# Forward first stages at every second place, and earlier statistics, norms and folds of the last slabs, in a fused Fourier-filter and GEGLU kernel on one Trainium2 core

## The chip, the core and the metric

The kernel runs on one core of a Trainium2 chip. The core has a matrix engine (TensorE, "PE" in the profile, with its weight loads as "PEld"), a vector engine (VectorE, "DVE"), an engine for activation functions (ScalarE, "ACT"), a general engine (GpSimd, "POOL") and SyncE ("SP"), which in this kernel issues every DMA. Each engine works through its own instructions in the order of the program and waits on semaphores for the others. The metric is the time of one execution in device microseconds (us), as the median of several runs.

## The reference

The input x has 2048 rows (S) of 640 values (D). It is normalized per row; one branch is a filter in the two-dimensional Fourier space of the whole array, the other a GEGLU feed-forward network with 1536 hidden values; the product of the two is added to x.

```python
def _A_ref(x, w_r, w_i):
    B, S, D = x.shape
    X = rfft2(x.astype(float32), axes=(-2, -1))
    X = X * (w_r + 1j * w_i)
    return irfft2(X, s=(S, D), axes=(-2, -1)).astype(bfloat16)

def _B_ref(x, w_gate, w_up, w_down):
    return (_gelu(x @ w_gate) * (x @ w_up)) @ w_down

x = A_x
xn = _layernorm(x, axis=-1)
s = _A_ref(xn, A_w_r, A_w_i)
g = _silu(_B_ref(xn, B_w_gate, B_w_up, B_w_down))
return x + s * g
```

## The kernel before

**Tiling.** The 2048 rows are cut into 16 slabs of 128 rows; slab n1 holds the rows 16 * n2 + n1. Four slabs make a group of 512 rows for the feed-forward part. The tile X holds all slabs (128 partitions, 16 slabs, 640 columns).

**Statistics, norms, folds (VectorE).** `stats(n1)` (line 190) is two `bn_stats` of 320 columns (L183) and one `bn_aggr` (L188) into the tile mva of the group; `half_stats` does one of the two halves. `root(n0, n)` adds epsilon on VectorE (ve, L197) and takes the power -0.5 on GpSimd (rst, L199). `norm(n1)` (L205) normalizes a slab in place; slabs 4 to 7 are normalized on ScalarE instead (`norm_act`, L453). The Fourier transform along the 640 columns uses symmetric and antisymmetric sums, which VectorE makes for four slabs at once: `fold_x` (two operations, L493 and L496), `fold_a` (two, L503), `fold_b` (two, L515, into the tile f), `fold_y` (three, L469, L476, L479, into the tile y). Their scratch lies in the tile GEN, on bytes that the construction of the Fourier tables uses before. The tiles f and y have two buffers each.

**Forward transform.** `slab_S1(n1)` (line 540) multiplies a slab's folds by the table Tfwd: four matmuls with f, one with y (L543, psum tile pz), and ScalarE copies the result into a buffer (CAST GEN<-pz, L545). `slab_D(n1)` (line 570) multiplies that copy by the table FT: six matmuls (L574, L576, psum tile pd); ScalarE copies them into the tile zd (L579, four buffers) and SyncE stores zd into the scratch ZDR in DRAM with two DMAs (L582). The psum tiles pz and pd take turns in two buffers of the pool psB. When all 16 slabs are stored, `load_B2` reads ZDR back in another order (ten DMAs, L600), and `s2_in` and `s2_out` apply the rest of the transform and the filter, whose two weights lie in W1 and W2. Half of W1 and of W2 is copied from the other half on the chip: `w_twin` (W<-W, L132, two DMAs for each), and `w_edge` halves their outer columns on GpSimd (L136). Then come the inverse transform (`slab_S1i`, `group_Di`) and the end (`finish`).

**Tables.** The Fourier tables are made on the chip. ScalarE loads another function table (`silu_table`, L335), then makes Tinv with two sine operations (`tinv_sin`, L339) and FT and FI (`ft_sin`, L369); SyncE transposes Tinv into Tfwd (`tfwd`). A smaller set, MG, is made by GpSimd (eight operations on the tile vg, L378), masked on VectorE (`mg_mask`, L417), put through a sine on ScalarE (sg, L421) and finished by GpSimd (`mg_build`); `mg_turn` transposes it into N1 and N2.

**Feed-forward part.** For each of 12 blocks t of 128 hidden values: the gate half (psum psg, five matmuls, L789), its gelu on ScalarE (ge, L793, three buffers), the up half (psum psu, five matmuls), and their product on VectorE (uT, L795). psg and psu have two buffers each. Then `down_third` (L814) multiplies uT by Wd, with the silu or tanh on ScalarE (L819, L822).

**Order.** Everything is issued in an order written out by hand. The list `back` has 144 steps; each step is a piece of the feed-forward part, and after each of them come the items that `put(step, ...)` has hung on it, in the order in which they were put. Steps 24 to 35 are the down matmuls of group 0 (three steps for each slab), steps 36 to 59 the gate and up halves of group 1 (even: gate of block (step - 36) / 2; odd: up), steps 60 to 71 the down matmuls of group 1. The table FA gives the step of each `slab_S1`; `slab_D` of a slab goes to the step of the next slab's `slab_S1`, ahead of it, or to two steps behind its own if that is sooner. `load_B2` hangs on step 60, the first burst of `s2_in` on step 67.

```python
for n1 in range(NS):
    put(min(FA[n1 + 1], FA[n1] + 2), slab_D, n1)
    put(FA[n1], slab_S1, n1)
```

In the trace step 24 begins at 35.34 us, step 36 at 50.82 us, step 48 at 68.51 us, step 60 at 85.73 us.

SyncE's order follows the same list: the stores of a slab stand at the step of its `slab_D`; the loads of W2 at 32, 35, 38 and 41, the transposes of the normalized slabs 8 to 11 (`slab_T`, L527) at 34, 37, 40 and 43, `mg_turn` at 45 and 46, the two `w_twin` of W2 at 47 and 48.

Of the kernel before, what the change touches and what calls it, by code (L numbers as in the profile page):

```python
# [32 lines left out]
def kernel(  # L33
# [40 lines left out]
    with tc.manual_schedule():  # L74
        build(nc, locals())


def build(nc, env):
# [792 lines left out]
    def put(s, *item):  # L871
        plan[s].append(item)
# [32 lines left out]
    put(31, mg_sin)  # L905
    put(31, mg_build)
    for at, *items in (
            (17, (stats, 8)), (18, (stats, 9)), (20, (stats, 10)), (22, (stats, 11), (root, 8, 4)),
            (24, (fold_x, 0, 4, 0), (fold_x, 0, 4, 1)), (25, (fold_a, 0, 4, 0), (fold_a, 0, 4, 1)),
            (26, (fold_b, 0, 4, 0), (fold_b, 0, 4, 1)), (27, (fold_y, 0, 4, 0), (fold_y, 0, 4, 1), (fold_y, 0, 4, 2)),  # L910
            (28, (fold_x, 4, 4, 0)), (29, (fold_x, 4, 4, 1)), (30, (fold_a, 4, 4, 0)),
            (31, (fold_a, 4, 4, 1), (fold_b, 4, 4, 0)), (32, (fold_b, 4, 4, 1), (fold_y, 4, 4, 0)),
            (33, (fold_y, 4, 4, 1), (fold_y, 4, 4, 2), (norm, 8)), (34, (norm, 9), (norm, 10), (norm, 11)), (35, (stats, 12)),
            (36, (stats, 13)), (37, (fold_x, 8, 4, 0)), (38, (fold_x, 8, 4, 1), (fold_a, 8, 4, 0)),
            (39, (fold_a, 8, 4, 1)), (40, (fold_b, 8, 4, 0), (fold_b, 8, 4, 1)), (41, (fold_y, 8, 4, 0)),
            (42, (fold_y, 8, 4, 1), (fold_y, 8, 4, 2), (half_stats, 14, 0)), (43, (half_stats, 14, 1)),
            (44, (stats, 15), (root, 12, 4)), (46, (norm, 12), (norm, 13)),
            (47, (norm, 14), (norm, 15)), (48, (fold_x, 12, 4, 0), (fold_x, 12, 4, 1)),
            (49, (fold_a, 12, 4, 0)), (50, (fold_a, 12, 4, 1), (fold_b, 12, 4, 0)), (51, (fold_b, 12, 4, 1)),
            (52, (fold_y, 12, 4, 0), (fold_y, 12, 4, 1)), (53, (fold_y, 12, 4, 2))):  # L920
        for it in items:
            put(at, *it)
    F0 = 30
    TURN = 45
    FA = (30, 32, 33, 35, 37, 39, 40, 42, 44, 46, 47, 49, 53, 55, 56, 58, 60)
    for n1 in range(NS):
        put(min(FA[n1 + 1], FA[n1] + 2), slab_D, n1)
        put(FA[n1], slab_S1, n1)
    z_end = F0 + 30
# [88 lines left out]
```

## Time and profile before

| | us |
|---|---|
| median of 3 runs (202.99 to 203.03) | 203.01 |
| the profiled execution | 203.26 |
| its span, first to last instruction | 201.5 |
| TensorE busy in the span | 193.4 |
| VectorE busy | 132.2 |
| ScalarE busy | 122.7 |
| GpSimd busy | 37.4 |
| steps 24 to 35, from 35.34 to 50.82 | 15.48 |
| from step 36 to `slab_D` of slab 15, 50.82 to 86.82 | 36.00 |
| DMA traffic, mean over the span | 161 GB/s |

The span leaves out what lies before the first and after the last instruction. An engine's busy time is the sum of its instructions; matmuls are pipelined and their ends are modelled, so for TensorE the distance between the starts of neighbouring groups tells more than a group's length. In a list in order of time, a row has the start, the length, the engine, the line, the operation, output and inputs, and, in brackets, how long the engine idled before it and which instruction ended the wait. The length of a DMA's row on SyncE is the time of its issue; when its data have landed is told by a separate figure, from issue to landing.

### The profile page before, as it was taken

To read this page: it belongs to the slowest core of one execution; us is meant where nothing else is said; L and a number is where in the kernel's file an instruction comes from. 1 tells how busy PE (TensorE), PEld (TensorE's weight loads), DVE (VectorE), ACT (ScalarE), POOL (GpSimd) and SP (SyncE) were. 2 spreads that over 40 slices of the span, in tenths; PEclk is the share of its full clock that TensorE was granted. 3 is DMA by queue.
4 is the path that set the end of the run, shared out by engine and by line. 5 is a ranking of instruction groups with operands and counts; after the bars stand their busy time and mean duration, and the time that the engine had idled before them with its cause. 6 is when DMAs were issued, how large, how long until landed. Compare 5 with 4: busy or idle time off the path is not lost.

```text
span 201.5 us, 4153 instructions
## 1 busy us (share of the span) xinstructions
PE 193.4 (96%) x1534; PEld 118.6 (59%) x1549; DVE 132.2 (66%) x320; ACT 122.7 (61%) x217; POOL 37.4 (19%) x62
## 2 busy tenths in 40 slices
PE   7889999999999997999999999999999999999993
PEld 5678854777555554576643433457765555556773
DVE  7876869799698784132665557423239786878673
ACT  2447657966967763733688787623564757476632
POOL 5427769999001000000000000000000000000000
PEclk9999999999999999999999999999999999999999
DMA  6999998656669537427982022249900406142512
GB/s 170 332 313 305 387 314 166 130 144 241 156 148 149 134 91 307 121 65 223 322 201 85 25 98 98 109 122 276 282 1 27 140 22 206 36 130 45 186 64 69
DMA packets 40325, 32.44 MB, mean 161 GB/s; under 512 B 15088, under 2 KB 38256, under 8 KB 40048
## 3 DMA queue, kind: packets, MB, share of 16 engines
q1 hardware_dynamic: 40304, 32.17, 55.8%
q8 instruction: 12, 0.20, 0.4%
q14 instruction: 9, 0.07, 0.2%
HBM read 19.03 MB, written 7.88 MB: 134 GB/s over the span
## 4 chain that ended last, share of the span: by engine, by line
PE 64%; DVE 1%; issue 1%; ACT 0%; DVEq 0%
PE psu L789 16%; PE psg L789 16%; PE psg L814 10%; PE psu L814 10%; PE pv L706 2%; PE pd L553 2%; PE pu L653 2%; PE px L626 2%; PE pd L574 1%; PE pd L557 1%; PE pz L543 1%; DVE uT L795 0%; PE pd L576 0%; DVE y L479 0%; ACT G L819 0%
## 5 line engine op out<-in xcount | busy, mean ns | idle before, releaser
L789 PE MATMUL psu<-xnT,Wu 128*128 128x512 bf16 (+2 forms) x289 | 61.0, 339 | 0.9 <-DVE uT L795 0.3
L789 PE MATMUL psg<-xnT,Wg 128*128 128x512 bf16 (+2 forms) x286 | 60.4, 338 | 0.8 <-ACT xnT L850 0.2
L795 DVE TENSOR_TENSOR uT<-psu,ge 128x512 bf16<-128x512 f32 (+2 forms) x59 | 34.4, 587 | 27.8 <-PE psu L789 22.1
L793 ACT ACTIVATE ge<-psg 128x512 bf16<-128x512 f32 (+2 forms) x59 | 30.5, 518 | 27.5 <-PE psg L789 24.6
L814 PEld LDWEIGHTS <-uT 128*128 128x128 bf16 x396 | 37.3, 98 | 14.3 <-issue 0.4
L789 PEld LDWEIGHTS <-Wu 128*128 128x128 bf16 x295 | 26.7, 98 | 23.3 <-issue 3.2
L789 PEld LDWEIGHTS <-Wg 128*128 128x128 bf16 x295 | 26.7, 98 | 21.7 <-issue 1.8
L814 PE MATMUL psg<-Wd,uT 128*128 128x320 bf16 (+1 forms) x204 | 30.7, 294 | 0.0
L814 PE MATMUL psu<-Wd,uT 128*128 128x320 bf16 (+1 forms) x192 | 28.7, 296 | 0.0
L638 DVE TENSOR_TENSOR X<-xs,W 128x972 bf16<-128x972 bf16 (+2 forms) x22 | 13.3, 648 | 10.2 <-ACT xs L634 9.3
L579 ACT CAST zd<-pd 128x660 bf16<-128x660 f32 x16 | 11.3, 706 | 5.5 <-PE pd L576 4.3
L183 DVE BATCH_NORM_STATS2 st<-X 128x6 f32<-128x320 bf16 x32 | 14.1, 477 | 0.4 <-DMA X<-in_A_x_dram 0.3
L708 ACT CAST W<-pv 128x640 bf16<-128x640 f32 x16 | 11.1, 695 | 5.0 <-PE pv L706 5.0
L731 ACT ACTIVATE W<-pd 128x960 bf16<-128x960 f32 (+2 forms) x14 | 10.1, 780 | 5.6 <-PE pd L557 5.5
L545 ACT CAST GEN<-pz 128x640 bf16<-128x640 f32 x16 | 11.2, 702 | 3.1 <-PE pz L543 3.1
L659 ACT CAST X<-pu 128x486 bf16<-128x486 f32 (+4 forms) x22 | 12.3, 558 | 0.3
L634 ACT CAST xs<-px 128x972 bf16<-128x972 f32 (+2 forms) x11 | 10.3, 937 | 2.9 <-PE px L626 2.9
L823 DVE SCALAR_TENSOR_TENSOR G<-th,psg 128x320 bf16<-128x320 f32 x8 | 3.9, 488 | 11.4 <-ACT th L822 11.4
L199 POOL TENSOR_TENSOR rst<-ve,mhalf 128x1 f32<-128x1 f32 (+1 forms) x7 | 5.4, 767 | 23.0 <-DVE ve L197 23.0
L737 DVE TENSOR_TENSOR W<-W 128x960 bf16<-128x960 bf16 (+1 forms) x12 | 6.9, 599 | 3.9 <-ACT W L731 3.8
L764 DVE TENSOR_TENSOR Yall<-Yall,G 128x640 bf16<-128x640 bf16 (+3 forms) x19 | 8.2, 434 | 1.6 <-ACT G L819 1.3
L765 DVE TENSOR_TENSOR Yall<-Yall,xt 128x640 bf16<-128x640 bf16 (+3 forms) x19 | 8.3, 439 | 0.7
(134 smaller groups left out, 207.9 us busy)
## 6 DMA issues: line engine op xcount, KB each, us to landing
W<-W SPq DMA_DIRECT2D x4, 642.0 KB, 5.1
ZDR<-zd SPq DMA_DIRECT2D x32, 80.2 KB, 2.6
xt<-in_A_x_dram SPq DMA_DIRECT2D x8, 320.0 KB, 3.8
UDR<-X SPq DMA_DIRECT2D x10, 240.8 KB, 2.5
out_dram<-Yall SPq DMA_DIRECT2D x14, 160.0 KB, 2.4
B<-ZDR SPq DMA_DIRECT2D x8, 240.8 KB, 4.2
W<-UDR SPq DMA_DIRECT2D x4, 481.5 KB, 6.6
X<-in_A_x_dram SPq DMA_DIRECT2D x3, 640.0 KB, 6.9
```

The lines of the kernel that those rows point to most:

```text
L183: nc.vector.bn_stats(out=st[:, k, :], in_=X[:, n1, 320 * k:320 * k + 320])
L545: nc.scalar.copy(out=Zt[n1], in_=pz)
L579: nc.scalar.copy(out=zd.rearrange("p c (q e) -> p c q e", e=10), in_=pd[:, :, 0:330].rearrange("p c (e q) -> p c q e", q=33))
L634: nc.scalar.copy(out=xs, in_=px[:, :, 0:n * w].rearrange("p k (h l) -> p k h l", l=w))
L638: nc.vector.tensor_tensor(out=pp[-1], in0=xs, in1=WT[:, :, h0:h0 + n, l0:l0 + w], op=ALU.mult)
L659: nc.scalar.copy(out=us[:, :, :, c0:c0 + (w + 1 - m) // 2], in_=pv[:, :, :, m:w:2])
L708: nc.scalar.copy(out=vs, in_=pv)
L731: nc.scalar.activation(out=eo[:, b, :, a0:a1].rearrange("p k a n -> p a k n"), in_=py[b][:, a0:a1], func=ACT.Copy, scale=(2.0 if silu[a0] ...
L789: nc.tensor.matmul(ps, lhsT=WT[:, c, t * P:(t + 1) * P], rhs=xnT[g][:, c, c0:c1_], start=(c == 0), stop=(c == 4))
L793: nc.scalar.activation(out=ges[t], in_=ps, func=ACT.Gelu_apprx_tanh)
L795: nc.vector.tensor_tensor(out=uT[g][:, t, c0:c1_], in0=ps, in1=ges[t], op=ALU.mult)
L814: nc.tensor.matmul(ph, lhsT=uT[g][:, t, j * P:(j + 1) * P], rhs=Wd[:, t, c0:c1_], start=(t == 0), stop=(t == NT - 1))
```

## The change

Three things in the hand-written order are altered; no instruction is added or taken away and no buffer changes.

- The table FA: up to slab 5 as before, then a `slab_S1` at every second step from 37 to 59 (before: pairs of neighbouring steps at 39 and 40, 46 and 47, 55 and 56, gaps of four at 49 to 53). `slab_D` follows by its rule; that of slab 15 stays at step 60.
- `stats(12)` moves from step 35 to step 23, after `root(8, 4)` and ahead of the folds of group 0; `stats(13)` to step 35, `stats(14)` and `stats(15)` to step 36 (before: 36, 42 to 43, 44). `root(12, 4)` moves from step 44 to 37, ahead of the folds of slabs 8 to 11.
- The folds of slabs 8 to 11 end at step 42 as before, with their parts spread otherwise; `norm(12)` to `norm(15)` move from steps 46 and 47 to 42 and 43, and the folds of slabs 12 to 15 from steps 48 to 53 to steps 44 to 49.

```diff
     for at, *items in (
-            (17, (stats, 8)), (18, (stats, 9)), (20, (stats, 10)), (22, (stats, 11), (root, 8, 4)),
+            (17, (stats, 8)), (18, (stats, 9)), (20, (stats, 10)), (22, (stats, 11), (root, 8, 4)), (23, (stats, 12)),
...
-            (33, (fold_y, 4, 4, 1), (fold_y, 4, 4, 2), (norm, 8)), (34, (norm, 9), (norm, 10), (norm, 11)), (35, (stats, 12)),
-            (36, (stats, 13)), (37, (fold_x, 8, 4, 0)), (38, (fold_x, 8, 4, 1), (fold_a, 8, 4, 0)),
-            (39, (fold_a, 8, 4, 1)), (40, (fold_b, 8, 4, 0), (fold_b, 8, 4, 1)), (41, (fold_y, 8, 4, 0)),
-            (42, (fold_y, 8, 4, 1), (fold_y, 8, 4, 2), (half_stats, 14, 0)), (43, (half_stats, 14, 1)),
-            (44, (stats, 15), (root, 12, 4)), (46, (norm, 12), (norm, 13)),
-            (47, (norm, 14), (norm, 15)), (48, (fold_x, 12, 4, 0), (fold_x, 12, 4, 1)),
-            (49, (fold_a, 12, 4, 0)), (50, (fold_a, 12, 4, 1), (fold_b, 12, 4, 0)), (51, (fold_b, 12, 4, 1)),
-            (52, (fold_y, 12, 4, 0), (fold_y, 12, 4, 1)), (53, (fold_y, 12, 4, 2))):
+            (33, (fold_y, 4, 4, 1), (fold_y, 4, 4, 2), (norm, 8)), (34, (norm, 9), (norm, 10), (norm, 11)),
+            (35, (stats, 13)), (36, (stats, 14), (stats, 15)),
+            (37, (root, 12, 4), (fold_x, 8, 4, 0), (fold_x, 8, 4, 1)), (38, (fold_a, 8, 4, 0)),
+            (39, (fold_a, 8, 4, 1), (fold_b, 8, 4, 0)), (40, (fold_b, 8, 4, 1)),
+            (41, (fold_y, 8, 4, 0), (fold_y, 8, 4, 1)), (42, (fold_y, 8, 4, 2), (norm, 12)),
+            (43, (norm, 13), (norm, 14), (norm, 15)), (44, (fold_x, 12, 4, 0)),
+            (45, (fold_x, 12, 4, 1), (fold_a, 12, 4, 0)), (46, (fold_a, 12, 4, 1)),
+            (47, (fold_b, 12, 4, 0), (fold_b, 12, 4, 1)), (48, (fold_y, 12, 4, 0)),
+            (49, (fold_y, 12, 4, 1), (fold_y, 12, 4, 2))):
...
-    FA = (30, 32, 33, 35, 37, 39, 40, 42, 44, 46, 47, 49, 53, 55, 56, 58, 60)
+    FA = (30, 32, 33, 35, 37, 39, 41, 43, 45, 47, 49, 51, 53, 55, 57, 59, 60)
```

On SyncE the stores of slab 5 thereby come behind the transpose of slab 10, those of slab 8 behind the second `mg_turn`, and those of slab 9 behind the two `w_twin` of W2 instead of ahead of them. On GpSimd the power of `root(12, 4)` comes ahead of `w_edge` of W1 instead of behind it.

## The prediction

> **What bounds the kernel now.** I read the page first. TensorE (PE) is busy for 96% of the span, no other engine for over two thirds, and the granted clock is 9 in every slice: only PE's own pauses can be won back. The profiled execution took 203.26 us, 1.8 us more than its span; the median of the runs shown is 203.01, so I work on the trace and take differences off the median.
>
> ```profile
> span 201.5 us, 4153 instructions
> PE 193.4 (96%) x1534; PEld 118.6 (59%) x1549; DVE 132.2 (66%) x320; ACT 122.7 (61%) x217; POOL 37.4 (19%) x62
> ```
>
> Then the busy time by stage (stretch, its length, PE busy with its count in brackets, ...). The third row, steps 36 to 60, holds nearly all that PE loses after the start, 1.57 us. The steps that the change rearranges lie there and in the row above.
>
> ```profile
> 35.34:50.82 15.48, 15.41 (x135) 11.34 (x134) 13.70 (x29) 11.32 (x21) 14.44 (x25) 1.00 0.63 175
> 50.82:86.82 36.00, 34.43 (x259) 19.28 (x261) 23.74 (x46) 24.73 (x40) 1.93 (x3) 1.00 0.60 152
> 86.82:101.20 14.38, 14.38 (x131) 9.70 (x128) 5.96 (x12) 7.17 (x14) 0.00 (x0) 1.00 0.74 215
> ```
>
> Then PE in order of time (start, length of the group, ..., in brackets the pause before it and who ended it).
>
> ```profile
> 66.45 1.24 PE L789 MATMUL psu<-xnT,Wu 128*128 128x512 bf16 x5
> 67.92 0.42 PE L574 MATMUL pd<-FT,GEN 128*128 128x132 bf16 x4 [0.22 <-ACT GEN L545]
> ...
> 75.88 0.39 PE L543 MATMUL pz<-Tfwd,f 128*128 128x128 bf16 x4
> 77.23 0.23 PE L543 MATMUL pz<-Tfwd,y 128*128 128x128 bf16 x1 [0.96 <-DVE y L479]
> 77.29 1.24 PE L789 MATMUL psg<-xnT,Wg 128*128 128x512 bf16 x5
> ```
>
> By the starts of neighbours, a gate or up half takes 1.08 us, a slab_D with the next slab_S1 0.58, eight down matmuls 1.09. From 50.82 (step 36) to 86.82 (slab_D of 15) there are 24 halves, 12 such pairs and eight down matmuls: 25.92 + 6.96 + 1.09 = 33.97. The other 2.03 us are pauses. Three stand where two first stages are one step apart: 0.24 before 57.63, 0.39 before 67.92, 0.20 before 81.32. There slab_D waits for ScalarE's copy of the slab just transformed, which follows the zd copy and a gelu. The fourth is the last fold of slabs 12 to 15 (y, L479): the fifth matmul of slab_S1 12 starts at 77.23, and the next half starts 1.13 us later than 75.88 + 0.28.
>
> **The change, part by part.** *Spacing.* With two steps between first stages from slab 5 on (2.74 us for two halves and a pair, against 1.87 us from one slab_D to the next where PE had waited for the copies, 79.45 to 81.32), the three short pauses go: 0.83 us. One step is left between slab_S1 15 (step 59) and slab_D 15 (60). Eight down matmuls take 1.09 us where a half takes 1.08, and no gelu precedes that zd copy, as at 81.32: a new pause of 0.20.
>
> *Norms and folds sooner.* VectorE gets the same work in another order. From 54.01 on, with the durations of its rows (folds of four slabs 5.2 us, four norms 1.5, an uT 0.6), the folds of 8 to 11 end at 61.5 and slab_S1 8 comes at 64.25; those of 12 to 15 end at 71.1 and slab_S1 12 comes at 75.2. The 1.13 us go, with 4 us to spare. The last uT is not pushed: VectorE is free before each. GpSimd's root of 12 to 15 (1.04 us) now stands ahead of w_edge of W1, which moves from 50.80 to some 56; W1 is first read at 96.28.
>
> *Statistics.* Each slab costs 1.04 us (30.31 to 31.35). Slab 12 goes to 36.34, into VectorE's 1.29 us wait for the Sin table; its x had landed by 31.7 (issued at 18.0, 13.7 to landing). It ends at 37.38, the fold starts at 37.71. Cover 0.33 us; without it each tenth is a tenth on PE, since slab_S1 0 already waits for the fold chain (y ends at 43.29, its matmul starts at 43.34).
>
> ```profile
> 35.73 0.69 DVE L795 TENSOR_TENSOR uT<-psu,ge 128x512 bf16<-128x512 f32 x1
> 37.71 0.96 DVE L493 TENSOR_TENSOR GEN<-X 128x1536 bf16<-128x1536 bf16 x1 [1.29 <-ACT Tinv L339]
> ...
> 54.01 0.69 DVE L795 TENSOR_TENSOR uT<-psu,ge 128x512 bf16<-128x512 f32 x1 [1.64 <-ACT ge L793]
> ```
>
> Slabs 13 to 15 run from 50.26 to 53.38 and still end before that uT, which waits for the gelu behind a table load. Both cost nothing.
>
> *GpSimd beside slab 12.* Its vg operations take 0.37 us while VectorE idles and 1.37 beside the folds:
>
> ```profile
> 37.46 0.37 POOL L378 TENSOR_SCALAR vg<-kr,n1x,phm 128x16 int32<-128x16 int32 x1
> 37.80 1.37 POOL L378 TENSOR_SCALAR vg<-kr,n1x,phs 128x16 int32<-128x16 int32 x1
> ```
>
> Three of them (36.78, 37.13, 37.46) now meet statistics. No row shows that pair at this size. Lower bound 0: the one-element operations beside statistics (34.50 to 35.38) take 0.19, as at 33.98 without. Upper bound: all three pushed among the folds, where others take 1.37 to 1.88, so 3.0 to 4.5 us. I take 0, the nearer row. The Trainium skill (SBUF — State Buffer, section "SBUF: two separate sides") says GpSimd is shut out of the port pair it shares with VectorE by operations with two SBUF inputs or in a two-port mode; statistics read one input, so by it the cost is 0 too, while the upper bound would stand if they held the pair. The trace agrees for the folds (1.37).
>
> *The stores.* This takes something back. Each slab_D issues two stores, ZDR<-zd, and SyncE issues everything in one order, without a pause from 66.64 to 80: it lags. The list moves store pair 5 behind a transpose and pair 8 behind the second N transpose, harmless (the zd copies that reuse their buffers, 9 and 12, come at 69.9 and 78.2; by the slowest landings of the rows around them, 4.8 and 2.7 us, the pairs are down by 69.1 and 76.7). But the two 642 KB W<-W copies (step 47/48) now stand ahead of pair 9, not behind it: they are issued 1.29 us sooner, at 74.65. Now pair 9 lands in 2.3 to 2.7 us; pair 10, right behind the copies, needs up to 5.9.
>
> ```profile
> 75.94 1.23 SPq L132 DMA_DIRECT2D W<-W x2
> 77.27 9.45 SPq L582 DMA_DIRECT2D ZDR<-zd x10
> ...
> DMA to landing us min/median/max: 3.3/4.8/6.3
> ...
> DMA to landing us min/median/max: 2.3/2.5/2.7
> ...
> DMA to landing us min/median/max: 4.1/5.2/5.9
> ```
>
> (The three last: the copies; the stores issued from 74 to 76; those from 77 to 80.5.) Pair 10 is issued at 77.27 and 78.26 and landed at 83.14 and 83.42. Pair 9 takes that place: 83.42 - 1.29 = 82.13. The zd tile has four buffers, so zd copy 13 waits for pair 9. It is due at 80.39 (slab_D 13, my sum) + 0.51 = 80.90, so it waits 1.2 us. Queued behind it on ScalarE are the copy of slab_S1 14, the gelu of step 58 and zd 14. The copy then ends at 82.15 + 0.60 + 0.70 = 83.45 and slab_D 14 starts at 83.52, due at 83.13: 0.39 us lost. The rest fits: the gelu ends at 84.05, zd 14 starts at 84.03, 0.51 behind slab_D 14, when pair 10 has long landed, and the last uT, done by 84.7, is read after 85.7.
> Bounds: 0 (SyncE's stretched issues, 2.01 us at 62.87 against 1.25 elsewhere and 0.45 idle before 65.96, come to 1.2 us; if they vanish in the new order, pair 9 lands at 80.9) and 1.2 (no slack on PE). I take 0.39, since the same DMA load stands behind those stretches. The Trainium skill (DMA: Bandwidth & Descriptors, section "Queues, rings and completion order") speaks against the change: each DMA engine takes descriptors in ring order, and a semaphore lands only after that engine's earlier writes, so a store behind the copies cannot overtake them. By it the loss stands; if stores could overtake, the sum would be 1.82. The trace agrees (last landings 82.85 for the copies, 83.14 for the store).
>
> *Behind step 60* nothing is moved. From slab_D 15 to the first burst PE has the same work (87.12 to 94.82), and stores, ten B loads and bursts hang on slab_D 15 as now; the first two loads land 3.0 us after 91.27, 0.5 before that burst.
>
> Sum: 0.83 + 1.13 - 0.20 - 0.39 = 1.37; by 33.97 us of work, with the rounding, 2.03 - 0.59 = 1.44. I take 1.4: a profiled time of 201.85, a median of 201.6.
>
> **The rivals.** *Stores in time* (24%): pair 9 lands before 81.74, nothing reaches PE: 1.82 off, 201.2. For it: the stretched issues; against: they go with the DMA load. *The wait passes whole* (13%): ScalarE's 1.2 us find no slack, as PE has only two buffers for pd and pz: 1.82 - 1.2 = 0.6 off, 202.4. Against it: without the wait that copy ends at 82.20, 0.9 us ahead of its use. *The last fold still late* (4%): the edit does not do what it says, because VectorE's uT's or the root hold up the folds by over 4 us: the 1.13 stay, about 202.7. *Slower, by GpSimd* (8%): statistics of slab 12 hold it, and vg ends 3.0 to 4.5 us after 44.56. ScalarE's sg (44.86) waits for VectorE's mask on vg, with zd 0 and the copy of slab_S1 1 behind it; slab_D 1 at 47.47 already waits 0.22 for that copy, so after some 0.5 us of ScalarE's slack PE loses 2.5 to 4.0. Less the gain: 204.1 to 205.6. It decides from a delay of 2 us.
>
> **How the numbers follow.** The forecast has 50%, 1% is unexplained. The first two rivals and the forecast are faster by over 0.2% (0.4 us, about what measuring this kernel can tell from no change): 0.87. The fold rival is the same, 0.04; the rest slower, 0.09. The range runs from 201.0 (stores in time, less the spread) to 202.4 (the wait whole).
>
> **What would show it.** PE without pauses over 0.1 us from step 38 to 57; slab_S1 12 near 75.2 and no wait for y; slab_D 14 waiting for ScalarE and zd 13 for a DMA; 0.2 before slab_D 15, which starts at 85.4. I am wrong if the fold at 37.71 or vg's end at 44.56 moves, or if zd 13 doesn't wait.

## The result and the profile after

The changed kernel takes 201.27 us (median of 6 runs, 201.22 to 201.80), the kernel before 203.02 (6 runs, 202.99 to 203.16). The ratio is 0.9915, with a 95% interval of 0.9904 to 0.9926: 1.75 us faster. That is inside the stated range, but 0.33 us below the forecast of 201.6 and next to the rival "stores in time" (201.2, 24%).

The page of the changed kernel, its first two lines:

```profile
span 199.4 us, 4150 instructions
PE 193.1 (97%) x1534; PEld 118.9 (60%) x1549; DVE 131.6 (66%) x320; ACT 123.1 (62%) x217; POOL 38.0 (19%) x62
```

The span fell by 2.1 us, more than the median. The stage table tells why (stretch, its length, then the busy time of PE, PEld, DVE, ACT and POOL, granted clock, DMA share and GB/s):

```profile
35.09:50.58 15.49, 15.42 (x136) 11.35 (x135) 14.71 (x32) 11.34 (x21) 14.42 (x25) 1.00 0.54 157
50.58:84.83 34.25, 33.96 (x259) 19.47 (x262) 22.26 (x43) 25.05 (x40) 2.61 (x3) 1.00 0.56 159
```

Step 24 begins at 35.09 instead of 35.34. Those 0.25 us lie ahead of everything that was changed and are no part of the gain: the start differs between executions (in a second trace of the changed kernel step 24 begins at 35.24), and the profiled execution of before stood 0.25 above its median. From step 36 to slab_D 15 the kernel now takes 84.77 - 50.58 = 34.19 us instead of 36.00: 1.81 less. TensorE's idle time there fell from 1.57 to 0.29 us. Behind slab_D 15, 114.6 us are left to the end of the span, as before (114.7).

TensorE in order of time, three places of that stage:

```profile
57.14 1.03 PE L789 MATMUL psu<-xnT,Wu 128*128 128x512 bf16 x4
58.22 0.41 PE L574 MATMUL pd<-FT,GEN 128*128 128x132 bf16 x4
...
74.98 0.39 PE L543 MATMUL pz<-Tfwd,f 128*128 128x128 bf16 x4
75.20 0.22 PE L543 MATMUL pz<-Tfwd,y 128*128 128x128 bf16 x1
...
81.82 1.24 PE L789 MATMUL psu<-xnT,Wu 128*128 128x512 bf16 x5
82.90 0.41 PE L574 MATMUL pd<-FT,GEN 128*128 128x132 bf16 x4
...
83.49 1.25 PE L814 MATMUL psg<-Wd,uT 128*128 128x320 bf16 x8
84.77 0.42 PE L574 MATMUL pd<-FT,GEN 128*128 128x132 bf16 x4
```

`slab_D` of slab 5 (slab_D 5 from here on, and so for the others) follows the half before it by exactly 1.08 us: the pause of 0.24 is gone, and so are the two like it. The y matmul of slab_S1 12 follows its neighbours by 0.22 us; before, it was 1.35. slab_D 14 starts 1.08 us after the half before it, on time. slab_D 15 comes 1.28 us after eight down matmuls that take 1.09: the new pause, 0.19.

ScalarE just ahead of slab_D 14, where the prediction expected a loss:

```profile
79.28 0.60 ACT L793 ACTIVATE ge<-psg 128x512 bf16<-128x512 f32 x1
81.49 0.71 ACT L579 CAST zd<-pd 128x660 bf16<-128x660 f32 x1 [1.61 <-DMA ZDR<-zd]
82.10 0.70 ACT L545 CAST GEN<-pz 128x640 bf16<-128x640 f32 x1
```

The copy into zd of slab 13 (zd copy 13) does wait for a store. It was due 0.51 us after slab_D 13 (80.16), at 80.67, so it is 0.82 late. The copy of slab_S1 14 behind it ends at 82.80, and slab_D 14 needs it at 82.90. The wait was just hidden, with some 0.04 us to spare after the 0.06 that lie between such a copy and its reader. So a lateness of about 0.86 us is covered here; the prediction had counted on nearly the same cover, but on a lateness of 1.2.

Two parts of the old pauses are gone (0.83 and 1.13), one is new (0.19), and their sum of 1.77 lies within 0.04 us of what the stage (1.81) and the median (1.75) show.

### The profile page after: what moved, and what is told of

It is laid out like the page before. It is cut to its first block, busy times and chain, and to the rows that moved or that the text cites. A ratio compares the mean times of both kernels' runs of the same rounds, so it can differ in the third digit from the quotient of the medians.

```text
span 199.4 us, 4150 instructions
## 1 busy us (share of the span) xinstructions
PE 193.1 (97%) x1534; PEld 118.9 (60%) x1549; DVE 131.6 (66%) x320; ACT 123.1 (62%) x217; POOL 38.0 (19%) x62
## 4 chain that ended last, share of the span: by engine, by line
PE 91%; DVE 4%; DMA 1%; issue 1%; ACT 1%; POOL 1%
PE psu L789 25%; PE psg L789 25%; PE psg L814 13%; PE psu L814 13%; PE pv L706 2%; PE pd L553 2%; PE pu L653 2%; PE pz L543 2%; PE pd L574 2%; PE px L626 2%; DVE st L183 1%; DMA X<-in_A_x_dram 1%; PE pd L557 1%; POOL rst L199 1%; DVE X L205 1%
## 5 line engine op out<-in xcount | busy, mean ns | idle before, releaser
L199 POOL TENSOR_TENSOR rst<-ve,mhalf 128x1 f32<-128x1 f32 (+1 forms) x7 | 6.0, 854 | 13.8 <-DVE ve L197 13.8
```

## The experiments

Each kernel is told by its edit against the changed kernel, unless said otherwise. Beside them the kernel before ran again, with medians of 203.15 (first four), 203.09 (next four) and 203.10 us (last two).

**One half of the change at a time.** The first has only the new places of the first stages, the second only the new order of statistics, norms and folds.

```diff
 # e1, against the kernel before
-    FA = (30, 32, 33, 35, 37, 39, 40, 42, 44, 46, 47, 49, 53, 55, 56, 58, 60)
+    FA = (30, 32, 33, 35, 37, 39, 41, 43, 45, 47, 49, 51, 53, 55, 57, 59, 60)
 # e2, against the changed kernel
-    FA = (30, 32, 33, 35, 37, 39, 41, 43, 45, 47, 49, 51, 53, 55, 57, 59, 60)
+    FA = (30, 32, 33, 35, 37, 39, 40, 42, 44, 46, 47, 49, 53, 55, 56, 58, 60)
```

> The kernel before with the new places of the forward first stages alone (statistics, norms and folds in their old order). If the two gains are coupled (TensorE runs ahead and meets the last fold of slabs 12 to 15): the three short pauses go, one of 0.2 us before slab_D 15 comes, and the wait for the last fold stays at about 0.9 of its 1.13 us, because VectorE's waits for up halves shrink as TensorE runs ahead: some 0.85 us off, 202.15 us. If the gains simply add: 0.83 - 0.20 = 0.63 off, 202.4 us, with the wait for the fold still 1.1 us. If the wait swallows all that spacing saves: 203.0 us.

Measured: 202.17 us (202.10 to 202.25), ratio 0.9946 (0.9929 to 0.9963). That is the number of the first case, 202.15. TensorE in order of time, at slab_S1 12:

```profile
75.16 0.39 PE L543 MATMUL pz<-Tfwd,f 128*128 128x128 bf16 x4
76.21 0.23 PE L543 MATMUL pz<-Tfwd,y 128*128 128x128 bf16 x1 [0.66 <-DVE y L479]
```

The next half starts at 76.28, 0.84 us late instead of 1.13. With TensorE ahead, VectorE waits less for the up halves (its uT's come sooner), and so the last fold comes sooner too, but it stays late.

> The changed kernel with the old places of the first stages: statistics, norms and folds sooner alone. The wait for the last fold (1.13 us) goes and the three short pauses (0.24, 0.39, 0.20) stay: 1.13 off, 201.9 us. Rival: the wait had given ScalarE and the stores time, so that a new pause stands behind slab 12, and less than 0.8 us are won.

Measured: 201.97 us (201.91 to 202.06), ratio 0.9938 (0.9923 to 0.9952). From step 36 (50.74) to slab_D 15 (85.60) it takes 34.86 us, 1.14 less than before: the fold's wait, to 0.01. The short pauses stand where they stood; this is the second of them:

```profile
67.84 0.42 PE L574 MATMUL pd<-FT,GEN 128*128 128x132 bf16 x4 [0.22 <-ACT GEN L545]
```

What follows: each half wins by itself, and they overlap. Against the 203.15 beside them the halves save 0.98 and 1.18, together 2.16; both at once save 1.75. The overlap that the trace shows is 0.29 us, the part of the fold's wait that spacing alone already shortens; the other 0.12 are of the size of the spread between sets of runs (203.02 and 203.15 for the same kernel).

**Is the wait for the stores hidden?** One kernel puts the W2 copies behind the stores of slab 9 again, another takes one of the four zd buffers away, so that each zd copy waits for the stores of three slabs earlier.

```diff
 # e3
-    for i, places in enumerate(((8, 9, 10, 11, 12, 13, 14, 15, 30, 31), (32, 32, 35, 35, 38, 38, 41, 41, 47, 48))):
+    for i, places in enumerate(((8, 9, 10, 11, 12, 13, 14, 15, 30, 31), (32, 32, 35, 35, 38, 38, 41, 41, 49, 50))):
 # e4
-        zd = work.tile([P, 2, 330], BF16, tag="zd", bufs=4, name="zd")
+        zd = work.tile([P, 2, 330], BF16, tag="zd", bufs=3, name="zd")
```

> The changed kernel with the two W2 copies at steps 49 and 50, so that the stores of slab 9 are ahead of them again. If the wait of zd copy 13 for those stores is hidden (in the changed kernel it starts 0.8 us late and TensorE does not pause): the wait goes from the trace and the time stays, 201.27 us within 0.1. If it costs TensorE something in most executions, as the prediction had it (0.39 us): 200.9 us.

Measured: 201.35 us (201.27 to 201.41), ratio 0.9906 (0.9892 to 0.9921). In its trace zd copy 13 starts at 80.69, 0.50 us after its slab_D, without a wait for a store. The saving, 1.80 us, is that of the changed kernel's first runs within the spread: in those, the wait cost nothing that can be told. (The changed kernel did not run beside this one, and the last experiment shows that the wait is not always hidden.)

> The changed kernel with three zd buffers instead of four. If the stores behind the W2 copies are what the zd copies wait for, with some 0.9 us of cover: zd copy 12 is due at 77.9 us and waits for the stores of slab 9, which land at 81.4: 3.5 us, of which 2.6 reach TensorE, 203.9 us. If those stores don't matter to the time: 201.3 us.

Measured: 204.09 us (9 runs, 203.63 to 205.43), ratio 1.0059 (1.0035 to 1.0084). ScalarE, then TensorE:

```profile
81.61 0.71 ACT L579 CAST zd<-pd 128x660 bf16<-128x660 f32 x1 [4.34 <-DMA ZDR<-zd]
...
82.97 0.41 PE L574 MATMUL pd<-FT,GEN 128*128 128x132 bf16 x4 [2.51 <-ACT GEN L545]
```

zd copy 12 waits for the stores behind the W2 copies, until 81.61. It would have come some 0.5 us after its slab_D, which started at 77.55, so it is 3.5 us late, and slab_D 13, due 2.74 us after its predecessor, starts 2.7 us late. That shows the mechanism of the prediction's store term, with its cover of about 0.9 us; in the changed kernel it is the size that was off.

**The statistics beside the table load.** One kernel takes those of slab 12 out of that place, another adds those of slab 13.

```diff
 # e5
-            (17, (stats, 8)), (18, (stats, 9)), (20, (stats, 10)), (22, (stats, 11), (root, 8, 4)), (23, (stats, 12)),
+            (17, (stats, 8)), (18, (stats, 9)), (20, (stats, 10)), (22, (stats, 11), (root, 8, 4)),
-            (35, (stats, 13)), (36, (stats, 14), (stats, 15)),
+            (35, (stats, 12), (stats, 13)), (36, (stats, 14), (stats, 15)),
 # e6
-            (17, (stats, 8)), (18, (stats, 9)), (20, (stats, 10)), (22, (stats, 11), (root, 8, 4)), (23, (stats, 12)),
+            (17, (stats, 8)), (18, (stats, 9)), (20, (stats, 10)), (22, (stats, 11), (root, 8, 4)), (23, (stats, 12), (stats, 13)),
-            (35, (stats, 13)), (36, (stats, 14), (stats, 15)),
+            (36, (stats, 14), (stats, 15)),
```

> The changed kernel with the statistics of slab 12 back at step 35, ahead of those of 13 to 15. If their new place brings nothing by itself (the four then end at some 54.2 us, 0.4 us behind the gelu that the first uT of group 1 waits for, and TensorE doesn't need that uT yet): 201.3 us, as the changed kernel. If the place beside the table load is part of the gain: slower by up to 1.0 us, 202.3 us.

Measured: 201.43 us (201.31 to 201.80), ratio 0.9922 (0.9910 to 0.9934). The change's ratio was 0.9915 (0.9904 to 0.9926): the place of slab 12 brings nothing that can be told from the spread.

> The changed kernel with the statistics of slab 13 also put beside the table load. Cover left there is 0.2 to 0.3 us, one slab costs 1.04: the folds start 0.7 us later, the wait of slab_S1 0 for its y fold grows by as much, 202.0 us. If that wait is not on the path: 201.3 us.

Measured: 201.97 us (201.93 to 202.06), ratio 0.9945 (0.9932 to 0.9958). TensorE at slab_S1 0, and GpSimd beside the second slab's statistics and beside the fold after them:

```profile
43.78 0.23 PE L543 MATMUL pz<-Tfwd,y 128*128 128x128 bf16 x1 [0.72 <-DVE y L479]
...
37.83 0.37 POOL L378 TENSOR_SCALAR vg<-kr,n1x,php 128x16 int32<-128x16 int32 x1
38.17 1.40 POOL L378 TENSOR_SCALAR vg<-kr,n1x,phs 128x16 int32<-128x16 int32 x1
```

Beyond the cover the folds start later one for one (38.16 instead of 37.46), and TensorE pays the same 0.7 us (the y matmul at 43.78 instead of 43.09). The slot holds one slab and no more.

**Less than two steps elsewhere.** Two places with one step of distance are left: slab_D 1 (step 33) and slab_D 15 (step 60).

```diff
 # e7
-    FA = (30, 32, 33, 35, 37, 39, 41, 43, 45, 47, 49, 51, 53, 55, 57, 59, 60)
+    FA = (30, 31, 33, 35, 37, 39, 41, 43, 45, 47, 49, 51, 53, 55, 57, 59, 60)
 # e8: the W2 copies of e3, and
+    FA = (30, 31, 33, 35, 37, 39, 41, 43, 45, 47, 49, 51, 53, 55, 57, 59, 61)
-    F0 = 30
+    F0 = 31
 # e9: e7 with the W2 copies of e3; e10: the changed kernel again
```

> The changed kernel with slab_S1 1 at step 31 instead of 32, so that the second slab_D also has two steps of distance. If one step of distance costs 0.2 us on TensorE wherever it stands: the pause ahead of slab_D 1 (47.22 us) goes, 201.05 us. If ScalarE, which has the silu and the sine of the small table to do there, is late anyway: 201.3 us.

Measured: 201.23 us (6 runs, 201.05 to 202.66, the others at most 201.57), ratio 0.9920 (0.9899 to 0.9940). slab_D 1 is on time (47.10), and slab_D 3 comes 17.50 us after step 24 instead of 17.64. But the wait of zd copy 13 now reaches TensorE: slab_D 14 starts at 82.83, where the half before it began at 81.69, 0.06 late. Too little is left to tell from the spread.

> The same with slab_D 15 at step 61 and all that hangs on it (B loads, bursts, inverse transform) one step later, and the W2 copies behind the stores of slab 9. If the last pause (0.2 us ahead of slab_D 15) goes too and the later steps have room: 200.85 us. If the end of the kernel has no room for a step more: 201.05 us or above.

Measured: 202.59 us (202.13 to 202.82), ratio 0.9965 (0.9952 to 0.9978): 1.7 us above what was hoped, and slower than the changed kernel, so the second case (201.05 or above) holds. The pause ahead of slab_D 15 is gone, but more is lost behind it. The first burst, on TensorE:

```profile
94.14 0.36 PE L626 MATMUL px<-B,MG 64*64 64x162 bf16 x2 [0.38 <-DMA B<-ZDR]
94.68 0.40 PE L626 MATMUL px<-B,MG 64*64 64x486 bf16 x3 [0.18 <-DMA B<-ZDR]
```

It now waits 0.56 us for the B loads. The step more is not the reason by itself, since the burst moved by a step as slab_D 15 did, and the first load is issued 4.1 us after slab_D 15 in both kernels; but the first two loads land 4.2 and 4.5 us after their issue, and 2.8 and 3.0 in the changed kernel. That uses up the 0.5 us of cover that the prediction had counted there; why they land later is not shown. More is lost at the end: the last product of the last slab is ready on VectorE at 198.10, 1.15 later than in the changed kernel, though TensorE's last matmuls come only 0.69 later, and from there to the end of the span it takes 0.45 us longer than in the changed kernel. The profiled execution was the slowest of the five; two of them took 202.13 and 202.15.

> The changed kernel with slab_S1 1 at step 31 and the W2 copies at steps 49 and 50, slab_D 15 and the B loads where they are. If the earlier slab_S1 1 is worth 0.15 us and the zd wait had eaten half of it again (slab_D 14 started 0.06 us late there): 0.15 us under the changed kernel, 201.1 us, with no pause over 0.1 us between 45 and 82 us. If the difference is no more than the spread: the same as the changed kernel beside it.

> The changed kernel itself once more, beside the kernel above: 201.3 us. Its zd copy 13 waits for the stores of slab 9 again; if slab_D 14 is on time within 0.1 us here too, the cover found in the first profile is not an accident of one execution.

Measured on one chip: e9 201.21 us (201.11 to 201.42), ratio 0.9908 (0.9895 to 0.9922); the changed kernel beside it 201.55 (201.39 to 201.58), ratio 0.9921 (0.9907 to 0.9934). In e9's trace no pause over 0.1 us is left between 45 and 82 us. In the changed kernel's second profile the wait does reach TensorE (ScalarE, then TensorE):

```profile
81.86 0.71 ACT L579 CAST zd<-pd 128x660 bf16<-128x660 f32 x1 [1.83 <-DMA ZDR<-zd]
...
81.97 1.24 PE L789 MATMUL psu<-xnT,Wu 128*128 128x512 bf16 x5
83.22 0.42 PE L574 MATMUL pd<-FT,GEN 128*128 128x132 bf16 x4
```

1.25 us from the half to slab_D 14 instead of 1.08: 0.17 lost. Put together, the traces with four zd buffers in which zd copy 13 waits for a store agree on the cover: late by 0.36 (e5), 0.53 (e6) and 0.82 us (the first profile), nothing is lost; late by 0.93 (e7), 0.06; late by 1.04 (here), 0.17. So some 0.87 us are covered. How late the stores land differs from trace to trace (0.82 and 1.04 us in two of the same kernel), and that the first profile kept 0.04 us was luck. e9 is 0.34 us under the kernel it ran beside; 0.22 us are won ahead of slab_D 3 (9.81 us after slab_S1 0, against 10.03) and 0.17 at slab_D 14. It has the lowest median of all kernels measured here, though the intervals of the two ratios overlap.

## Why the prediction came out as it did

- *Spacing, 0.83 less 0.20.* Right. The three pauses are gone, the one ahead of slab_D 15 is 0.19.
- *The last fold, 1.13.* Right. The last fold of slabs 12 to 15 ends at 70.9, slab_S1 12 comes at 75.0: 4 us to spare, as worked out. e2 isolates it at 1.14.

```profile
70.52 0.43 DVE L479 TENSOR_TENSOR y<-y,X 128x512 bf16<-128x512 bf16 x1
```

- *Statistics, nothing.* Right. VectorE still idles ahead of the fold and of the first uT:

```profile
37.07 0.21 DVE L188 BATCH_NORM_AGGREGATE mva<-st 128x2 f32<-128x12 f32 x1
37.46 0.96 DVE L493 TENSOR_TENSOR GEN<-X 128x1536 bf16<-128x1536 bf16 x1 [0.19 <-ACT Tinv L339]
...
53.77 0.69 DVE L795 TENSOR_TENSOR uT<-psu,ge 128x512 bf16<-128x512 f32 x1 [0.64 <-ACT ge L793]
```

  The row shows 0.19 us of idle time ahead of the fold. Counted from where another instruction can start (0.13 behind the aggregate's start, as in e6) the cover was 0.26 rather than 0.33, since the aggregate starts 0.98 us after its statistics and not 0.91 as elsewhere. e6 shows what lies beyond it: another 0.99 us of statistics moved the fold by 0.70.
- *GpSimd, nothing.* Right, and settled: the three vg operations beside the statistics (36.53, 36.88, 37.21) take 0.37 each, and the next one meets the fold. The last vg operation ends at 44.32, which is 44.56 less the earlier start of this execution.

```profile
37.21 0.37 POOL L378 TENSOR_SCALAR vg<-kr,n1x,phm 128x16 int32<-128x16 int32 x1
37.54 1.37 POOL L378 TENSOR_SCALAR vg<-kr,n1x,phs 128x16 int32<-128x16 int32 x1
```

  The rival "slower, by GpSimd" falls with it. The Trainium skill (SBUF — State Buffer, section "SBUF: two separate sides") has only operations with two SBUF inputs or in a two-port mode shut GpSimd out; the trace agrees, with 0.37 beside statistics and 1.37 beside a fold.
- *The stores, 0.39.* The mechanism was right, the size was not: the loss is 0 in the first profile and 0.17 in the second, and the forecast had 0.39. This is the mis-sized term; of the signs that the prediction named, "slab_D 14 waiting for ScalarE" shows in the second profile only. SyncE's transpose of slab 10 in the kernel before and in the changed one; then, in the changed one, its row for the copies, their landing, the landing of the stores behind them, and who waited for these:

```profile
62.87 2.01 SPq L527 DMA_TRANSPOSE xnT<-X  x1
...
61.09 1.24 SPq L527 DMA_TRANSPOSE xnT<-X  x1
...
73.43 1.24 SPq L132 DMA_DIRECT2D W<-W  x2
...
DMA to landing us min/median/max: 5.8/6.2/6.7
...
DMA to landing us min/median/max: 5.1/5.7/6.3
...
  ACT zd L579: 1.6, 1
```

  The prediction put the copies at 74.65, or 74.40 less the 0.25 of this execution. They came 1.0 us sooner. Of these, 0.77 are the transpose of slab 10, issued in 1.24 us and not in 2.01: the stretched issue, which the prediction kept, was not carried over to the new order. But the copies then took longer to land, 5.8 and 6.7 us instead of 3.3 and 6.3, and the stores landed at 81.39, only 0.5 sooner than the 81.88 that were forecast (82.13 less the 0.25), and 0.1 inside the limit of the rival "stores in time" (81.74 less the 0.25). In e7 the copies were issued at 74.67 and the stores behind them landed at 81.37; in the second profile of the changed kernel at 73.80 and at 81.7. So the step that failed is "Pair 9 takes that place: 83.42 - 1.29 = 82.13": the landing did not keep its distance to the issue.

  One conclusion in that paragraph, that a store behind the copies cannot overtake them, goes further than its source: the Trainium skill (DMA: Bandwidth & Descriptors, section "Queues, rings and completion order") orders a semaphore only behind the earlier writes of the same DMA engine. The traces agree with the conclusion even so: in the changed kernel the later copy landed at 80.8, the two stores at 81.1 and 81.4.

The forecast without its store term is 1.76 to 1.83 us; 1.75 was measured. So the gains and the new pause came out as they were worked out; the one loss that the forecast added did not reach TensorE in the first runs, which is what the rival "stores in time" said; that it stayed hidden by 0.04 us was luck.

## What to carry to other kernels

When one engine is busy 96% of the time, list its pauses one by one with their releasers, and check that work plus pauses give the stretch; here that sum held to 0.07 us, and the gain could be read from it. Two edits can shorten the same wait: the spacing alone took 0.29 us off the wait for the last fold, which the earlier folds remove whole, so the savings of the halves are not simply added. When an order is rearranged, follow each queue that it passes through, and ask how far a landing time can be trusted: with the stores of one slab behind two large copies, one execution of this kernel stayed 0.04 us clear of a loss, and another lost 0.17 us.

## What the runs showed of the hardware

The same two 642 KB copies on the chip landed 3.3 and 6.3 us after issue in the kernel before, 5.8 and 6.7 us when issued 2.5 us earlier in the changed one, and 4.0 and 5.5 us in e7. In the last two cases the stores behind them landed within 0.05 us of each other (81.39 and 81.37), although the issues were 1.2 us apart; in the second profile of the changed kernel they landed at 81.7. An 80 KB store issued right behind the copies occupied SyncE for 1.25 to 1.45 us in the changed kernel and 0.95 to 1.34 in the kernel before, where most stores issued at other places take 0.6. What sets the landing was not isolated by any run and stays open.
